# An inner Strassen level for product 5 of the first matrix multiplication, four units at a time, in the second token block of a fused MLP kernel

## The chip, the cores and the metric

The kernel runs on one core of one Trainium2 chip. Times are device microseconds (us) of that core. Each run of the kernel has a state: "slow" when the core is granted a lower clock or when the run is more than 1.5% above the fastest run of the same kernel. The medians quoted are of all runs.

Names in the profiles: PE is TensorE, which does the matrix multiplications ("matmuls"); PEld is the loading of its weights; DVE is VectorE, ACT ScalarE, POOL GpSimd, SP SyncE. A small q after a name (SPq) marks the queue of an engine. PSUM is the memory, in banks, in which the products of matmuls are summed; SBUF holds the operands. f16 and f32 are number formats of 16 and 32 bits. L625 is line 625 of that run's kernel.

A ratio of two kernels is the mean time of the fast runs of one over the mean time of the fast runs of the other in the same rounds, so it is not quite the ratio of the medians quoted beside it.

## The reference, cut to what matters

```python
B, S, D, F = 1, 2048, 1024, 3584
def reference(x, w1, b1, w2, b2):
    y = _layernorm(x, axis=-1)
    h = _gelu(jnp.einsum("bsd,df->bsf", y, w1) + b1)      # "matmul 1"
    return jnp.einsum("bsf,fd->bsd", h, w2) + b2           # "matmul 2"
```

All inputs are bf16. The kernel treats the 2048 tokens as two blocks of 1024 (block 0 and block 1).

## The kernel before

The kernel already uses Strassen's method in Winograd's form: a product of two matrices, each cut in 2x2 blocks, is made from seven block products instead of eight. In matmul 1 the blocks are halves of the token block (512 tokens), halves of K (D = 1024, so four tiles of 128), and pairs of 128-column slices of F. One such pair is a "unit" (14 units); two units are a "chunk" (7 chunks), whose weights are loaded together.

The seven products of a unit accumulate in three PSUM banks where they can. Product 5 is the odd one: it belongs to two of the four outputs, so it is copied out of PSUM once and then added twice, by `w6` and by `c7`.

```python
SEQ1 = (1, 5, 6, 2, 7, 3, 4)
OPER1 = {1: ("A11", (0, 0)), 2: ("A12", (1, 0)), 3: ("S4", (1, 1)), 4: ("A22", 4),
         5: ("S1", 1), 6: ("S2", 2), 7: ("S3", 3)}        # token operand, weight operand (number n: the sum Tn)

def w1_sums(s, c, prio):                 # T1..T4 of one chunk, on VectorE
    ...
    if n > 1:                            # T1 and T3 in one instruction of 2048 elements
        T1 = T3 = add("DVE", cost2(2 * KH * 2 * P), lambda e: e.tensor_tensor(
            out=t1_sb[:, n % 2, 0:3:2]..., in0=raw[:, :, :, 1, :], in1=raw[:, 0]..., op=ALU.subtract), ...)
    ...

def mm1_unit(s, c, v, T, t0):
    ...
    P1 = prod(1, ())                     # each prod: KH = 4 matmuls of 128x512
    o1 = snap(1, P1, b0 if fork else s1, pt[6] - SLOT)
    P5 = prod(5, ())
    o5 = snap(5, P5, s5, pt[3] - SLOT)   # product 5: PSUM -> SBUF, f32
    P6 = prod(6, (o1,))                  # bank b0: P1 + P6
    o2 = add("DVE", 0.7, lambda e: e.tensor_tensor(     # "w6": bank b5 = b0 + P5
        out=ps[:, b5.k, :], in0=ps[:, b0.k, :], in1=sn_sb[:, s5.k, :], op=ALU.add), (P6, o5), ...)
    P2 = prod(2, (o1,) if fork else ())
    ...
    P7 = prod(7, (P6, o2))               # bank b0: P1 + P6 + P7; waits for w6
    c22 = fin(7, P7, o5, s5, pt[4] - SLOT, ())          # "c7": b0 + P5
    gelu(22, sn(s5), c22, ...)
    P3 = prod(3, (o2,))                  # bank b5: output 12
    ...
    P4 = prod(4, (P7, c22))              # bank b0: output 21
```

Matmul 2 of both blocks uses a second, inner level of the same method for most of its products, with matmuls of 128x256; the change carries that idea into matmul 1. All instructions are listed first and then put in a fixed order, engine by engine, by a list scheduler in the kernel's own code. So one added instruction can move many others, and each engine then runs its queue strictly in that order.

Of the kernel before, what the change touches and what calls it, by code (L numbers as in the profile page):

```python
# [5 lines left out]
ACT = mybir.ActivationFunctionType  # L6
ALU = mybir.AluOpType
BF16 = mybir.dt.bfloat16
FP16 = mybir.dt.float16
# [14 lines left out]
P = 128  # L24
# [61 lines left out]
class Planner:  # L86
# [8 lines left out]
    def add(self, *a, **k):  # L95
        o = Op(*a, **k)
        self.ops.append(o)
        return o
# [139 lines left out]
def bass_standalone__mixer_channel_mlp__prompt_kernel(  # L238
# [24 lines left out]
    with ExitStack() as es:  # L263
# [27 lines left out]

        x16 = x_sb[:, :, :].bitcast(FP16)
        w1_16 = w1_sb[:, :, :, :].bitcast(FP16)
        h = {q: h_sb[:, n] for n, q in enumerate((11, 12, 21, 22))}
# [199 lines left out]
        def dma_T(s, i, prio, gate):  # L494
# [6 lines left out]
            y_in[(s, i)] = res  # L501

        opnd = {}
        h_war = {}
# [26 lines left out]

        cost2 = lambda n: 0.15 + n / 1920
        t1_use = {}
        SEQ1 = (1, 5, 6, 2, 7, 3, 4)
# [5 lines left out]
        def w1raw(n, kh, ev, v=None):  # L540
            t = w1_sb[:, n % N_W1, kh * KH:(kh + 1) * KH, :].rearrange("p k (v e c) -> p k v e c", v=2, e=2)
            return t[:, :, :, ev, :] if v is None else t[:, :, v, ev, :]

        def w1_sums(s, c, prio):
            n = s * NC + c
            tv = lambda k: t1_sb[:, n % 2, k - 1].rearrange("p k (v c) -> p k v c", v=2)
            ld = w1_ld[(s, c)]
            war = t1_use.get(n - 2, {})

            def tt(k, x0, x1, deps):  # L550
                return add("DVE", 0.65, lambda e: e.tensor_tensor(out=tv(k), in0=x0, in1=x1, op=ALU.subtract),  # L551
                           [*deps, *war.get(k, ())], prio + 0.5 * k, f"w1T{k}_{s}_{c}")

            if n > 1:
                raw = w1_sb[:, n % N_W1].rearrange("p k c -> p (k c)").rearrange("p (j v e c) -> p j v e c", j=2, e=2, c=P)
                T1 = T3 = add("DVE", cost2(2 * KH * 2 * P), lambda e: e.tensor_tensor(
                    out=t1_sb[:, n % 2, 0:3:2].rearrange("p a k (v c) -> p a (k v) c", c=P), in0=raw[:, :, :, 1, :],
                    in1=raw[:, 0].rearrange("p v e c -> p e v c"), op=ALU.subtract),
                    [*ld, *war.get(1, ()), *war.get(3, ())], prio + 0.5, f"w1T13_{s}_{c}")
            else:  # L560
                T1 = tt(1, w1raw(n, 0, 1), w1raw(n, 0, 0), (ld[0],))
                T3 = tt(3, w1raw(n, 1, 1), w1raw(n, 0, 1), ld)
            T2 = tt(2, w1raw(n, 1, 1), tv(1), (ld[1], T1))
            T4 = tt(4, w1raw(n, 1, 0), tv(2), (ld[1], T2))
            w1_use[n] = list(dict.fromkeys((T1, T2, T3, T4)))
            return {1: T1, 2: T2, 3: T3, 4: T4}

# [31 lines left out]

        def mm1_unit(s, c, v, T, t0):  # L600
            n = s * NC + c
# [5 lines left out]
            if not fork:  # L607
                hold.update({1: b0, 2: b1})
                b0.seeded = False
            s1, s5 = Holder(snaps), Holder(snaps)  # L610
            pt = {p: t0 + 2 * k * SLOT for k, p in enumerate(SEQ1)}
            nm = f"{s}_{u}"
            mine = {}

# [31 lines left out]

            def gelu(q, src, o, at, frees):
                f = 2 * u + q % 10 - 1
                r = h_ok[(s, q, u)] = add("ACT", 0.70, lambda e: e.activation(  # L649
                    out=h[q][:, u, :], in_=src(), func=ACT.Gelu_apprx_tanh, bias=b1_sb[:, f:f + 1], scale=1.0),  # L650
                    [o, b1c, *h_war.get((s, q), ()), *(h_head.get((q, u), ()) if s == 0 else ())], at, f"g{q}_{nm}",
                    frees=frees)
                return r
# [3 lines left out]
            o1 = snap(1, P1, b0 if fork else s1, pt[6] - SLOT)  # L657
            P5 = prod(5, ())
            o5 = snap(5, P5, s5, pt[3] - SLOT)
            P6 = prod(6, (o1,))  # L660
            o2 = add("DVE", 0.7, lambda e: e.tensor_tensor(  # L661
                out=ps[:, b5.k, :], in0=ps[:, b0.k, :], in1=sn_sb[:, s5.k, :], op=ALU.add), (P6, o5), pt[7] - SLOT,
                f"w6_{nm}")
            P2 = prod(2, (o1,) if fork else ())
# [5 lines left out]
            P7 = prod(7, (P6, o2))  # L670
            c22 = fin(7, P7, o5, s5, pt[4] - SLOT, ())
            gelu(22, sn(s5), c22, pt[4] + 4 * SLOT, (s5,))
            P3 = prod(3, (o2,))
# [5 lines left out]
            for p, k in ((5, 1), (6, 2), (7, 3), (4, 4)):  # L679
                t1_use[n].setdefault(k, []).append(mine[p])  # L680
            return list(mine.values())
# [23 lines left out]
        def flat(*a):  # L705
            return list(dict.fromkeys(o for x in a for l in x[1] for o in l))

        def uniq(*a):
            return list(dict.fromkeys(o for l in a for o in l))

# [528 lines left out]
        for s in range(NSB):  # L1239
            last = []  # L1240
            for c in range(NC):
                n = s * NC + c
                t0 = base1[s] + c * 14 * SLOT
                if n:
                    T = w1_sums(s, c, t0 - 2 * SLOT)
                    for v in range(2):
                        last += mm1_unit(s, c, v, T, t0 + v * SLOT)
                m = n + N_W1
# [88 lines left out]
```

## Time and profile before

| | before |
|---|---|
| median of 5 runs | 341.14 us (340.67 to 439.31; the run of 439.31 us is slow) |
| span of the profiled run | 338.9 us |
| TensorE (PE) busy | 332.5 us, 98% |
| VectorE (DVE) busy | 274.1 us, 81% |
| ScalarE (ACT) busy | 165.2 us, 49% |

The first lines of the profile page of the kernel before: span, then busy time, share of the span and number of instructions of each engine (PEld is the loading of weights into TensorE).

```profile
span 338.9 us, 5855 instructions
## 1 busy us (share of the span) xinstructions
PE 332.5 (98%) x2347; PEld 219.1 (65%) x2347; DVE 274.1 (81%) x350; ACT 165.2 (49%) x275; POOL 21.4 (6%) x47
```

A busy PE alone does not say that PE is the limit. The chain of work that ended last does: it is followed back from the last instruction, at each step to what released it. The columns are start, duration, and what ran; "x384" is the number of instructions merged in a line. This is the chain of the kernel before from 29.32 us on; its last two lines, 0.02 us of issue and 0.42 us of VectorE, are left out.

```profile
29.32 69.93 PE ps L625 x324
99.25 32.10 PE ps L898 x294
131.34 24.17 PE ps L823 x112
155.52 19.87 PE ps L898 x182
175.39 1.73 PE ps L625 x8
177.11 1.53 PE ps L898 x14
178.64 82.88 PE ps L625 x384
261.52 73.36 PE ps L898 x672
334.88 1.54 PE ps L903 x14
```

Each line starts where the line above ends, and in this part no other engine and no transfer appears. L625 is matmul 1 (128x512 matmuls), L898 the inner products of matmul 2 (128x256). The stage that the change touches is the line at 178.64 us: 384 matmuls in 82.88 us, 215.8 ns each. The 672 narrower ones after it take 73.36 us, 109.2 ns each. Two narrow ones cost 218.4 ns, almost the same as a wide one, so the width is nearly free and the number of multiplications sets the time.

The other engines in that stage, from the view of busy time by stretches (in brackets the number of instructions):

```profile
178.00:261.50 83.50, 83.50 (x392) 38.13 (x391) 52.83 (x64) 48.51 (x78) 0.00 (x0) 1.00 0.63 210
```

The columns after the stretch and its length are busy time of PE, PEld, DVE, ACT and POOL, then granted clock, DMA share and GB/s. VectorE is 52.83 us busy of 83.50 us.

### The profile page before, as it was taken

Reading aid. Unit: us, or ns where it says so; the run is one execution under the profiler, and the core shown is the slowest. Engines: PE = TensorE matmul, PEld = TensorE weight load, DVE = VectorE, ACT = ScalarE, POOL = GpSimd, SP = SyncE. Lnnn points to the kernel's source line nnn. Section 1 sums busy time; section 2 is a strip of 40 time slices with the busy share of each in tenths; the row PEclk is TensorE's granted clock in tenths of the full one; section 3 lists DMA queues with packets and bytes.
Section 4 is the critical chain, followed back from the end, with each engine's and each line's share of the span. In section 5 each row is a group of like instructions: output and inputs, shape, how many; then the busy total and the mean of one; then the engine's idle time right before and its main releaser. Section 6 shows DMA issues by size and latency. Waiting matters only on the chain.

```text
span 338.9 us, 5855 instructions
## 1 busy us (share of the span) xinstructions
PE 332.5 (98%) x2347; PEld 219.1 (65%) x2347; DVE 274.1 (81%) x350; ACT 165.2 (49%) x275; POOL 21.4 (6%) x47
## 2 busy tenths in 40 slices
PE   5999999999999999999999999999999999999997
PEld 4986444444458886447884444444445888888885
DVE  4789997989899989999995578387547989989954
ACT  3865975764688878212113575576475331101110
POOL 2320120000011403200000000000000000000000
PEclk9999999999999999999999999999999999999999
DMA  7739999897999999999593747949931999998112
GB/s 244 254 71 307 355 351 292 281 380 245 311 337 294 339 286 384 195 336 400 191 349 96 276 148 260 339 145 371 315 110 39 349 354 356 348 363 267 62 35 91
DMA packets 79204, 89.18 MB, mean 263 GB/s; under 512 B 14026, under 2 KB 66122, under 8 KB 78666
## 3 DMA queue, kind: packets, MB, share of 16 engines
q1 hardware_dynamic: 79034, 88.69, 81.0%
q8 instruction: 18, 0.29, 0.4%
q10 hardware_dynamic: 144, 0.13, 0.1%
q14 instruction: 8, 0.07, 0.0%
HBM read 61.81 MB, written 24.38 MB: 254 GB/s over the span
## 4 chain that ended last, share of the span: by engine, by line
PE 97%; DMA 1%; DVE 1%; ACT 0%; POOL 0%; issue 0%
PE ps L625 46%; PE ps L898 37%; PE ps L823 7%; PE ps L583 5%; PE ps L481 1%; DMA x_sb<-in_x_dram 1%; PE ps L903 0%; DVE st_sb L396 0%; ACT yw_sb L488 0%; POOL rstd_sb L403 0%; DVE x_sb L406 0%; DVE o_sb L787 0%; DVE mv_sb L399 0%; DVE vpe_sb L400 0%; PE ps L384 0%
## 5 line engine op out<-in xcount | busy, mean ns | idle before, releaser
L625 PE MATMUL ps<-yw_sb,t_sb 128*128 128x512 f16 x416 | 96.3, 379 | 0.0
L625 PE MATMUL ps<-yw_sb,w_sb 128*128 128x512 f16 x312 | 74.0, 379 | 0.0
L625 PEld LDWEIGHTS ps<-yw_sb,t_sb 128*128 128x128 f16 x416 | 40.7, 98 | 48.6
L649 ACT ACTIVATE h_sb<-ps,b_sb 128x512 f16<-128x512 f32 x76 | 50.7, 684 | 31.8 <-PE ps L625 30.5
L625 PEld LDWEIGHTS ps<-yw_sb,w_sb 128*128 128x128 bf16 x312 | 30.4, 98 | 36.1
L698 DVE TENSOR_TENSOR h_sb<-h_sb 128x2048 f16<-128x2048 f16 (+2 forms) x36 | 38.2, 1085 | 0.3 <-ACT h_sb L649 0.3
L807 ACT COPY sn_sb<-ps 128x512 f32<-128x512 f32 x27 | 15.8, 584 | 31.2 <-PE ps L898 16.3
L787 DVE TENSOR_TENSOR sn_sb<-ps,sn_sb 128x512 f32<-128x512 f32 x35 | 24.0, 687 | 7.9 <-PE ps L898 7.6
L898 PE MATMUL ps<-w2a_sb,h_sb 128*128 128x256 f16 (+1 forms) x252 | 30.1, 273 | 0.0
L807 ACT COPY ps<-sn_sb 128x512 f32<-128x512 f32 x12 | 7.0, 589 | 46.2 <-PE ps L898 45.6
L643 DVE TENSOR_TENSOR sn_sb<-ps,sn_sb 128x512 f32<-128x512 f32 x28 | 19.1, 689 | 12.3 <-PE ps L625 12.2
L661 DVE TENSOR_TENSOR ps<-ps,sn_sb 128x512 f32<-128x512 f32 x26 | 18.0, 697 | 12.7 <-PE ps L625 12.4
L898 PEld LDWEIGHTS ps<-w2a_sb,h_sb 128*128 128x128 f16 x252 | 24.7, 98 | 3.7
L787 DVE TENSOR_TENSOR o_sb<-ps,sn_sb 128x512 bf16<-128x512 f32 (+1 forms) x29 | 19.4, 669 | 6.7 <-PE ps L898 3.9
L823 PE MATMUL ps<-w2a_sb,h_sb 128*128 128x512 f16 x112 | 24.3, 379 | 0.0
L649 ACT ACTIVATE h_sb<-sn_sb,b_sb 128x512 f16<-128x512 f32 x28 | 19.9, 715 | 8.9 <-DVE sn_sb L643 8.9
L898 PE MATMUL ps<-w_sb,t_sb 128*128 128x256 f16 x196 | 23.4, 273 | 0.0
L551 DVE TENSOR_TENSOR t_sb<-w_sb,t_sb 128x1024 f16<-128x1024 bf16 x26 | 17.9, 689 | 4.4 <-PE ps L625 3.9
L898 PEld LDWEIGHTS ps<-w_sb,t_sb 128*128 128x128 f16 x196 | 19.2, 98 | 2.2
L823 PEld LDWEIGHTS ps<-w2a_sb,h_sb 128*128 128x128 f16 x112 | 10.9, 98 | 13.0 <-DMA w2a_sb<-w_sums 0.3
L638 ACT COPY sn_sb<-ps 128x512 f32<-128x512 f32 x24 | 14.1, 586 | 8.6 <-PE ps L625 8.5
L583 PE MATMUL ps<-yw_sb,w_sb 128*128 128x128 f16 x256 | 17.0, 230 | 0.3 <-ACT yw_sb L488 0.3
(107 smaller groups left out, 428.6 us busy)
## 6 DMA issues: line engine op xcount, KB each, us to landing
w_sb<-in_w_dram SPq DMA_DIRECT2D x28, 512.0 KB, 5.4
x_sb<-in_w_dram SPq DMA_DIRECT2D x21, 256.0 KB, 4.6
w_sums<-x_sb SPq DMA_DIRECT2D x21, 256.0 KB, 4.8
w2a_sb<-w_inner_sums SPq DMA_DIRECT2D x12, 448.0 KB, 8.4
x_sb<-in_x_dram SPq DMA_DIRECT2D x15, 256.0 KB, 5.4
w2a_sb<-in_w_dram SPq DMA_DIRECT2D x2, 1792.0 KB, 9.4
w_inner_sums<-w_sb SPq DMA_DIRECT2D x4, 896.0 KB, 5.1
x_sb<-w_sums SPq DMA_DIRECT2D x2, 1792.0 KB, 9.1
```

Source lines behind the costliest of these rows:

```text
L551: return add("DVE", 0.65, lambda e: e.tensor_tensor(out=tv(k), in0=x0, in1=x1, op=ALU.subtract), [*deps, *war.get(k, ())], prio + 0.5 * k, ...
L583: fn = [(lambda e, b=b, hb=hold[f], f=f, k=k, t=t: e.matmul(ps[:, hb.k, t * P:(t + 1) * P], lhsT=lhs[:, k, f * P:(f + 1) * P], rhs=yop[f"A ...
L625: fn = [(lambda e, k=k: e.matmul(ps[:, hold[p].k, :], lhsT=lhs[:, k, :], rhs=yop[yo][:, k, :], start=(first and k == 0), stop=(k == KH - 1 ...
L638: return e.copy(out=dst, in_=src) if o_.eng == "ACT" else e.tensor_copy(dst, src)
L643: return add("DVE", 0.69, lambda e: e.tensor_tensor(out=sn_sb[:, hold_s.k, :], in0=ps[:, hold[p].k, :], in1=sn_sb[:, hold_s.k, :], op=ALU. ...
L649: r = h_ok[(s, q, u)] = add("ACT", 0.70, lambda e: e.activation(out=h[q][:, u, :], in_=src(), func=ACT.Gelu_apprx_tanh, bias=b1_sb[:, f:f ...
L661: o2 = add("DVE", 0.7, lambda e: e.tensor_tensor(out=ps[:, b5.k, :], in0=ps[:, b0.k, :], in1=sn_sb[:, s5.k, :], op=ALU.add), (P6, o5), pt[ ...
L698: o = add("DVE", cost2(w * dst.shape[-1]), lambda e, k0=k0, k1=k1: e.tensor_tensor(out=dst[:, k0:k1, :], in0=a[0][:, k0:k1, :], in1=b[0][: ...
L787: plus = lambda e, out, x, y: e.tensor_tensor(out=out, in0=x, in1=y, op=ALU.add)
L807: return act(lambda e: e.copy(out=out(), in_=src()), deps, at - 5, name, **k)
L823: fn = [(lambda e, k=k, t=t: e.matmul(ps[:, banks_[t].k, :], lhsT=a[0][:, k, t * P:(t + 1) * P], rhs=b[0][:, k, :], start=(first and k == ...
L898: fn = [(lambda e, k=k, j=j: e.matmul(ps[:, bank[r].k, j * HI:(j + 1) * HI], lhsT=x[0][:, k, j * P:(j + 1) * P], rhs=y[0][:, k, :], start= ...
```

## The change

In block 1, the last six chunks are taken in three pairs. For each pair (four units, "group") product 5 is computed as one larger product with an inner Winograd level over halves of F (the two chunks), of K (two of the four tiles) and of tokens (256 of 512). Before, a group's product 5 is 4 units x 4 tiles = 16 matmuls of 128x512, which is the work of 32 of 128x256. After, it is 7 sub-products x 4 = 28 of 128x256. For this T1 of both chunks is needed earlier, four sums of T1 blocks (`gS`) and four sums of S1 blocks (`yi`, in three instructions, once) are added on VectorE, and the seven sub-products leave PSUM by five copies on ScalarE and two additions on VectorE, instead of four copies.

```diff
+        GROUPED = {(1, c): (0, (c - 1) % 2) for c in range(1, NC)}
+        LEAD = 6.0
...
-            if n > 1:
+            if n > 1 and (s, c) not in GROUPED:        # grouped chunks: T1 and T3 apart
...
+        def mm1_y_sums(s, yo, prio):                   # once: sums of the token operand S1
...
+        def mm1_group(s, c, p, yo, t0, free_y):
...
+            def tt(m, x, y, op, deps, **k):
+                return add("DVE", cost2(QK * QN), lambda e: e.tensor_tensor(out=S_(m), in0=x(), in1=y(), op=op), deps,
+                           t0 - 4 + 0.2 * m, f"gS{m}_{nm}", **k)
...
+            def sub(r, deps, first=False, frees=()):
+                (xo, dx), (yv, dy) = XO[r], Y[r]
+                fn = [(lambda e, k=k, v=v: e.matmul(
+                    ps[:, bank[r].k, v * QN:(v + 1) * QN], lhsT=xo()[:, k, v * P:(v + 1) * P], rhs=yv()[:, k, :],
+                    start=(first and v == k == 0), stop=(k == QK - 1), skip_group_check=True), ())
+                    for v in range(2) for k in range(QK)]
+                subs[r] = add("PE", CS, fn, ...)
...
+            sub(1, (), True)
+            sub(5, (), True)
+            f1 = cp(...)                               # ScalarE copies f1, k5, k2, r11, r21; VectorE additions r22, r12
+            k5 = cp(...)
+            sub(6, (f1,))
...
-            P5 = prod(5, ())
-            o5 = snap(5, P5, s5, pt[3] - SLOT)
+            if G is None:
+                P5 = prod(5, ())
+                o5 = (snap(5, P5, s5, pt[3] - SLOT),)
+            else:
+                o5 = G[1][gi]                          # w6 and c7 read the group's result
```

More of the change, by code (lines that the diff above doesn't have):

```diff
@@ L292, in bass_standalone__mixer_channel_mlp__prompt_kernel @@
         x16 = x_sb[:, :, :].bitcast(FP16)
+        sn16 = sn_sb[:, :, :].bitcast(FP16)
         w1_16 = w1_sb[:, :, :, :].bitcast(FP16)
@@ L501, in dma_T, with uniq @@
             y_in[(s, i)] = res
+        def uniq(*a):
+            return list(dict.fromkeys(o for l in a for o in l))
         opnd = {}
@@ L542, in w1raw, with w1_t1 @@
             return t[:, :, :, ev, :] if v is None else t[:, :, v, ev, :]
+        T1_of = {}
+        def w1_t1(s, c, prio):
+            n = s * NC + c
+            T1_of[(s, c)] = add("DVE", 0.65, lambda e: e.tensor_tensor(
+                out=t1_sb[:, n % 2, 0].rearrange("p k (v c) -> p k v c", v=2), in0=w1raw(n, 0, 1), in1=w1raw(n, 0, 0),
+                op=ALU.subtract), [w1_ld[(s, c)][0], *t1_use.get(n - 2, {}).get(1, ())], prio, f"w1T1_{s}_{c}")
         def w1_sums(s, c, prio):
@@ L560, in w1_sums @@
             else:
-                T1 = tt(1, w1raw(n, 0, 1), w1raw(n, 0, 0), (ld[0],))
+                T1 = T1_of.get((s, c)) or tt(1, w1raw(n, 0, 1), w1raw(n, 0, 0), (ld[0],))
                 T3 = tt(3, w1raw(n, 1, 1), w1raw(n, 0, 1), ld)
@@ L598, in mm1_plain @@
                                 f"g_{c}_{i}_{f}", frees=(hold[f],))
-        def mm1_unit(s, c, v, T, t0):
+        mm1_y = {}
+        QK, QN = KH // 2, 2 * P
+        def mm1_y_sums(s, yo, prio):
+            hold = Holder(snaps, 2)
+            flat_ = lambda: sn16[:, hold.k:hold.k + 2, :].rearrange("p a b -> p (a b)")
+            blk = lambda m: flat_()[:, m * QK * QN:(m + 1) * QK * QN].rearrange("p (k c) -> p k c", c=QN)
+            w = yop[yo].rearrange("p (j k) n -> p j k n", j=2)
+            dep = uniq(*opnd[s][yo])
+            o13 = add("DVE", cost2(2 * QK * QN), lambda e: e.tensor_tensor(
+                out=flat_()[:, 0:2 * QK * QN].rearrange("p (j k c) -> p j k c", j=2, c=QN), in0=w[:, :, :, QN:],
+                in1=w[:, 0].rearrange("p k (j c) -> p j k c", j=2), op=ALU.subtract), dep, prio, f"yi13_{s}", alloc=hold)
+            t2 = add("DVE", cost2(QK * QN), lambda e: e.tensor_tensor(
+                out=blk(2), in0=w[:, 1, :, QN:], in1=blk(0), op=ALU.subtract), (o13,), prio + 0.1, f"yi2_{s}")
+            t4 = add("DVE", cost2(QK * QN), lambda e: e.tensor_tensor(
+                out=blk(3), in0=w[:, 1, :, 0:QN], in1=blk(2), op=ALU.subtract), (t2,), prio + 0.2, f"yi4_{s}")
+            q = lambda l, j: (lambda: w[:, l, :, j * QN:(j + 1) * QN])
+            mm1_y[(s, yo)] = hold, {1: (q(0, 0), dep), 2: (q(1, 0), dep), 3: (q(1, 1), dep), 4: (lambda: blk(3), [t4]),
+                                    5: (lambda: blk(0), [o13]), 6: (lambda: blk(2), [t2]), 7: (lambda: blk(1), [o13])}
@@ new lines, in mm1_group, with cp, pl_ @@
+        def mm1_group(s, c, p, yo, t0, free_y):
+            nm = f"{p}g_{s}_{c}"
+            hold_y, Y = mm1_y[(s, yo)]
+            X, dX = {}, {}
+            for i in range(2):
+                n = s * NC + c + i
+                for l in range(2):
+                    X[(i, l)] = t1_sb[:, n % 2, 0, l * QK:(l + 1) * QK, :]
+                    dX[(i, l)] = [T1_of[(s, c + i)]]
+            hs = Holder(snaps, 2)
+            S_ = lambda m: sn16[:, hs.k:hs.k + 2, :].rearrange("p a b -> p (a b)")[
+                :, m * QK * QN:(m + 1) * QK * QN].rearrange("p (k c) -> p k c", c=QN)
+            def tt(m, x, y, op, deps, **k):
+                return add("DVE", cost2(QK * QN), lambda e: e.tensor_tensor(out=S_(m), in0=x(), in1=y(), op=op), deps,
+                           t0 - 4 + 0.2 * m, f"gS{m}_{nm}", **k)
+            x = lambda i, l: (lambda: X[(i, l)])
+            s1 = tt(0, x(1, 0), x(1, 1), ALU.add, dX[(1, 0)], alloc=hs)
+            s2 = tt(1, lambda: S_(0), x(0, 0), ALU.subtract, (s1, *dX[(0, 0)]))
+            s3 = tt(2, x(0, 0), x(1, 0), ALU.subtract, (*dX[(0, 0)], *dX[(1, 0)], s1))
+            s4 = tt(3, x(0, 1), lambda: S_(1), ALU.subtract, (s2, *dX[(0, 1)]))
+            XO = {1: (x(0, 0), dX[(0, 0)]), 2: (x(0, 1), dX[(0, 1)]), 3: (lambda: S_(3), [s4]), 4: (x(1, 1), dX[(1, 1)]),
+                  5: (lambda: S_(0), [s1]), 6: (lambda: S_(1), [s2]), 7: (lambda: S_(2), [s3])}
+            c0, c2, c5 = Holder(banks), Holder(banks, seeded=True), Holder(banks)
+            bank = {1: c0, 6: c0, 7: c0, 4: c0, 2: c2, 5: c5, 3: c5}
+            subs = {}
+            at = {r: t0 + 1.0 * k for k, r in enumerate(SEQ1)}
+            CS = 4 * MM256
+            def sub(r, deps, first=False, frees=()):
[4 more added lines that the diff above has]
+                    for v in range(2) for k in range(QK)]
+                subs[r] = add("PE", CS, fn, uniq(deps, dx, dy), at[r], f"G{r}_{nm}", alloc=bank[r] if first else None,
+                              frees=frees)
+            q = lambda h_: ps[:, h_.k, :]
+            g = Holder(snaps, 4)
+            row = lambda i, j: sn_sb[:, g.k + 2 * i + j, :]
+            def cp(out, src, deps, a, name, **k):
+                return add("ACT", 0.6, lambda e: e.copy(out=out(), in_=src()), deps, a - 3, f"{name}_{nm}", **k)
+            def pl_(dst, b, deps, a, name, **k):
+                return add("DVE", 0.69, lambda e: e.tensor_tensor(out=dst(), in0=b(), in1=dst(), op=ALU.add), deps, a - 3,
+                           f"{name}_{nm}", **k)
+            sub(1, (), True)
+            sub(5, (), True)
+            f1 = cp(lambda: q(c2), lambda: q(c0), (subs[1],), at[1], "f1", alloc=c2)
+            k5 = cp(lambda: row(1, 1), lambda: q(c5), (subs[5],), at[5], "k5", alloc=g)
+            sub(6, (f1,))
+            k2 = cp(lambda: row(0, 1), lambda: q(c0), (subs[6], k5), at[6], "k2")
+            sub(2, (f1,))
+            r11 = cp(lambda: row(0, 0), lambda: q(c2), (subs[2], k5), at[2], "r11", frees=(c2,))
+            sub(7, (k2,))
+            r22 = pl_(lambda: row(1, 1), lambda: q(c0), (subs[7], k5), at[7], "r22")
+            sub(3, (k5,))
+            r12 = pl_(lambda: row(0, 1), lambda: q(c5), (subs[3], k2), at[3], "r12", frees=(c5,))
+            sub(4, (r22,), frees=(hs, hold_y) if free_y else (hs,))
+            r21 = cp(lambda: row(1, 0), lambda: q(c0), (subs[4], k5), at[4], "r21", frees=(c0,))
+            for i, use in ((0, (subs[1], subs[2], s2, s3, s4)), (1, (subs[4], s1, s3))):
+                t1_use.setdefault(s * NC + c + i, {}).setdefault(1, []).extend(use)
+            return g, {0: (r11, r12), 1: (r22, r21)}, list(subs.values())
@@ L601, in mm1_unit @@
+        def mm1_unit(s, c, v, T, t0, G=None):
             n = s * NC + c
@@ L610, in mm1_unit, with v5, b5v @@
             s1, s5 = Holder(snaps), Holder(snaps)
+            if G is not None:
+                gi = GROUPED[(s, c)][1]
+                b5.seeded = True
+            def v5():
+                if G is None:
+                    return sn_sb[:, s5.k, :]
+                return sn_sb[:, G[0].k + 2 * gi:G[0].k + 2 * gi + 2, v * QN:(v + 1) * QN]
+            def b5v(h_):
+                return ps[:, h_.k, :] if G is None else ps[:, h_.k, :].rearrange("p (j c) -> p j c", j=2)
             pt = {p: t0 + 2 * k * SLOT for k, p in enumerate(SEQ1)}
             nm = f"{s}_{u}"
+            if G is not None:
+                pt[1] -= 3 * SLOT
             mine = {}
@@ L645, in fin, with gelu @@
                     (o, so), at, f"c{p}_{nm}", frees=frees)
-            def gelu(q, src, o, at, frees):
+            def gelu(q, src, o, at, frees, form=None):
                 f = 2 * u + q % 10 - 1
+                dst = h[q][:, u, :] if form is None else h[q][:, u, :].rearrange(form, j=2)
                 r = h_ok[(s, q, u)] = add("ACT", 0.70, lambda e: e.activation(
-                    out=h[q][:, u, :], in_=src(), func=ACT.Gelu_apprx_tanh, bias=b1_sb[:, f:f + 1], scale=1.0),
+                    out=dst, in_=src(), func=ACT.Gelu_apprx_tanh, bias=b1_sb[:, f:f + 1], scale=1.0),
                     [o, b1c, *h_war.get((s, q), ()), *(h_head.get((q, u), ()) if s == 0 else ())], at, f"g{q}_{nm}",
@@ L657, in mm1_unit @@
             o1 = snap(1, P1, b0 if fork else s1, pt[6] - SLOT)
-            P5 = prod(5, ())
-            o5 = snap(5, P5, s5, pt[3] - SLOT)
+            if G is None:
+                P5 = prod(5, ())
+                o5 = (snap(5, P5, s5, pt[3] - SLOT),)
+            else:
+                o5 = G[1][gi]
             P6 = prod(6, (o1,))
             o2 = add("DVE", 0.7, lambda e: e.tensor_tensor(
-                out=ps[:, b5.k, :], in0=ps[:, b0.k, :], in1=sn_sb[:, s5.k, :], op=ALU.add), (P6, o5), pt[7] - SLOT,
-                f"w6_{nm}")
+                out=b5v(b5), in0=b5v(b0), in1=v5(), op=ALU.add), (P6, *o5), pt[7] - SLOT,
+                f"w6_{nm}", alloc=b5 if G is not None else None)
             P2 = prod(2, (o1,) if fork else ())
@@ L670, in mm1_unit @@
             P7 = prod(7, (P6, o2))
-            c22 = fin(7, P7, o5, s5, pt[4] - SLOT, ())
-            gelu(22, sn(s5), c22, pt[4] + 4 * SLOT, (s5,))
+            if G is None:
+                c22 = fin(7, P7, o5[0], s5, pt[4] - SLOT, ())
+                gelu(22, sn(s5), c22, pt[4] + 4 * SLOT, (s5,))
+            else:
+                c22 = add("DVE", 0.69, lambda e: e.tensor_tensor(out=v5(), in0=b5v(b0), in1=v5(), op=ALU.add),
+                          (P7, o2), pt[4] - SLOT, f"c7_{nm}")
+                g22 = gelu(22, v5, c22, pt[4] + 4 * SLOT, (), "p (j c) -> p j c")
+                G[3].append(g22)
+                if len(G[3]) == 4:
+                    g22.deps += [o for o in G[3][:-1]]
+                    g22.frees = (G[0],)
             P3 = prod(3, (o2,))
@@ L679, in mm1_unit @@
             for p, k in ((5, 1), (6, 2), (7, 3), (4, 4)):
-                t1_use[n].setdefault(k, []).append(mine[p])
+                if p in mine:
+                    t1_use[n].setdefault(k, []).append(mine[p])
             return list(mine.values())
@@ L706, in flat @@
             return list(dict.fromkeys(o for x in a for l in x[1] for o in l))
-        def uniq(*a):
-            return list(dict.fromkeys(o for l in a for o in l))
         tq_ok = {r: [] for r in range(4)}
@@ L1244, in bass_standalone__mixer_channel_mlp__prompt_kernel @@
                 if n:
+                    if (s, c) in GROUPED and GROUPED[(s, c)][1] == 0:
+                        w1_t1(s, c, t0 - LEAD - 2)
+                        w1_t1(s, c + 1, t0 - LEAD - 1.9)
+                        if (s, "S1") not in mm1_y:
+                            mm1_y_sums(s, "S1", t0 - LEAD - 2)
+                        g_, ok_, subs_ = mm1_group(s, c, 5, "S1", t0 - LEAD, (s, c + 2) not in GROUPED)
+                        G = (g_, ok_, subs_, [])
+                        last += subs_
                     T = w1_sums(s, c, t0 - 2 * SLOT)
                     for v in range(2):
-                        last += mm1_unit(s, c, v, T, t0 + v * SLOT)
+                        last += mm1_unit(s, c, v, T, t0 + v * SLOT, G if (s, c) in GROUPED else None)
                 m = n + N_W1
```

## The prediction

> **What bounds the kernel now.** TensorE. The page's first part gives PE 332.5 us busy of a 338.9 us span (98%); the chain that ended last is 97% PE. Its listing in order of time has no gap in the stage concerned: 384 matmuls of 128x512 take 82.88 us from 178.64 us, 215.8 ns each, and the 672 of 128x256 after them take 73.36 us, 109.2 ns each. The Trainium skill ("TensorE: Matmul & The Clock Gate", back-to-back issue gap) states N/2.4 GHz plus about 2.5 ns when warm; this trace agrees at both widths, and the granted clock is 1.0. So halving the width costs almost nothing (2 x 109.2 = 218.4 against 215.8), and only fewer multiplications shorten the stage. From 178 to 262 us VectorE is 53.3 us busy and ScalarE 49.0 us.
>
> **What the change removes.** In block 1 six of the seven chunks, in three groups of four units, stop computing product 5 as 16 matmuls of 128x512 (16 x 215.8 ns = 3.45 us per group) and compute seven sub-products of four 128x256 matmuls (28 x 109.2 ns = 3.06 us): 0.395 us per group, 1.19 us in all. Four copies of product 5 out of PSUM per group go too (0.59 us each, mostly ScalarE).
>
> **What it adds and moves.** Per group: four 128x512 f16 sums on VectorE (estimate 0.42 us each, from 0.69 us at 1024 and 1.22 us at 2048 elements), two 0.69 us PSUM additions, two splits of the fused T1/T3 sum (0.3 us), five ScalarE copies of 0.58 us. Once: three token sums, about 1.5 us. VectorE gains about 11.6 us in all, to some 65 of 83 us; ScalarE about 0.5 us a group.
>
> **What lies on the critical path.** The PE saving wholly; the rest only where a new wait appears. By the new order of instructions, sub-products are interleaved with the preceding units' products, so nearly each has a 0.86 us product between it and what it needs. Two tight places, laid out by hand with the trace's durations:
> - First group: VectorE is never idle from 173 to 180 us in the old trace. I get the first operand sum ready about 2 us early.
> - Second and third groups: the later chunk's weights are requested when a buffer comes free, land 4 to 5 us later, and then T1 and four sums stand in VectorE's queue ahead of the "w6" additions which product 7 needs. I get 0.2 to 0.5 us of slack; a wait of up to 0.5 us per group is possible, none is my central case.
>
> The stage after is bound by PE too, so the gain should pass through.
>
> **Prediction.** 341.13 - 1.19 + 0.15 (stalls) = about 340.1 us; range 339.2 to 341.4. Faster by over 2%: 0.01; within 2%: 0.97; slower by over 2%: 0.02.
>
> **What would show it.** Right: in the chain, the same gap-free stretch with 48 matmuls of 128x512 replaced by 84 of 128x256, about 1.2 us shorter; 128x256 intervals near 109 ns; VectorE up by about 11 us there; the last stage equally long. Wrong: VectorE or ScalarE steps, or a weight load, in the chain between sub-products or before product 7, with idle PE time ahead.
>
> **What would make it wrong.** A late weight load; the in-order VectorE queue holding back w6; sub-products costing more than 109 ns per matmul at their borders; the last stage limited by transfers; scatter between runs, 0.5 us in the old one.

## The result, and the profile after

| | before | after |
|---|---|---|
| median | 341.14 us (5 runs) | 340.19 us (5 runs, 338.94 to 340.49) |
| ratio | | 0.9967, 95% interval 0.9944 to 0.9990 |
| the stage (PE chain) | 82.88 us | 81.69 us |

The page of the changed kernel begins:

```profile
span 338.5 us, 5977 instructions
## 1 busy us (share of the span) xinstructions
PE 330.9 (98%) x2383; PEld 221.8 (66%) x2383; DVE 282.4 (83%) x376; ACT 167.0 (49%) x279; POOL 22.6 (7%) x47
```

The chain that ended last in the changed kernel, from the second load wait of block 0 on. L745 is what L625 was, L1029 what L898 was, and L670 is the new sub-products.

```profile
125.23 8.04 DMA w2a_sb<-w_sums
133.27 0.05 issue
133.32 22.84 PE ps L954 x105
...
179.27 5.18 PE ps L745 x24
184.46 0.44 PE ps L670 x4
184.89 0.86 PE ps L745 x4
185.75 0.44 PE ps L670 x4
...
218.19 13.81 PE ps L745 x64
232.01 0.87 PE ps L670 x8
...
241.97 18.99 PE ps L745 x88
260.96 73.36 PE ps L1029 x672
```

The stage runs from 179.27 to 260.96 us, 81.69 us: 1.19 us less than 82.88 us. It still holds nothing but PE. A sub-product of four matmuls takes 0.44 us, two in a row 0.87 us, where 4 x 109.2 ns is 0.437 us; so a border between wide and narrow matmuls costs nothing to be seen. The last stage is 73.36 us in both kernels, so the gain passes through to the end.

The spans of the two profiled runs differ by only 0.4 us, because the stage starts at 179.27 us here and at 178.64 us in the profile before. That difference lies in block 0, where both kernels have the same instructions in the same order on every engine (the two traces first differ at 176.63 us, on VectorE); most of it is the first three lines above, a load for matmul 2 that landed late (TensorE waited 0.4 us for it). This is why the stage, and not the span of one run, is the measure in what follows.

VectorE and ScalarE in the stage of the changed kernel, same columns as before:

```profile
178.00:261.00 83.00, 83.00 (x434) 42.27 (x433) 61.72 (x90) 50.89 (x83) 0.00 (x0) 1.00 0.63 214
```

VectorE rises from 52.83 to 61.72 us, ScalarE from 48.51 to 50.89 us. These two stretches begin 0.64 and 1.27 us before the stage; between the ends of the stage itself VectorE rises from 52.27 to 60.84 us and ScalarE from 48.53 to 50.49 us. How close this comes to costing time is seen at the second group. The timeline of the changed kernel (start, duration, engine, line, operation, output and inputs), cut to VectorE and to product 7 on PE:

```profile
205.36 0.69 DVE L554 TENSOR_TENSOR t_sb<-w_sb 128x1024 f16<-128x1024 bf16 x1 [0.25 <-DMA w_sb<-in_w_dram]
206.09 0.42 DVE L652 TENSOR_TENSOR sn_sb<-t_sb 128x512 f16<-128x512 f16 x1
206.54 0.43 DVE L652 TENSOR_TENSOR sn_sb<-sn_sb,t_sb 128x512 f16<-128x512 f16 x1
206.89 0.42 DVE L652 TENSOR_TENSOR sn_sb<-t_sb 128x512 f16<-128x512 f16 x1
207.22 0.42 DVE L652 TENSOR_TENSOR sn_sb<-t_sb,sn_sb 128x512 f16<-128x512 f16 x1
207.56 1.29 DVE L785 TENSOR_TENSOR ps<-ps,sn_sb 128x512 f32<-128x512 f32 x2
...
208.94 1.89 PE L745 MATMUL ps<-yw_sb,t_sb 128*128 128x512 f16 x8
```

T1 of the later chunk waits a quarter of a microsecond for its weights, then come the four sums (0.42 us each), then the two `w6` additions (0.69 us each, overlapping). The first ends at 208.25 us, and the product 7 that needs it starts at 208.94 us: 0.69 us of slack. In the first and third groups it is 0.73 and 0.45 us.

### The profile page after: what moved, and what is told of

Read it like the earlier page. It is cut to its first block, busy times and chain, and to the rows that moved or that the text cites. A ratio compares the mean times of both kernels' runs of the same rounds, so it can differ in the third digit from the quotient of the medians.

```text
span 338.5 us, 5977 instructions
## 1 busy us (share of the span) xinstructions
PE 330.9 (98%) x2383; PEld 221.8 (66%) x2383; DVE 282.4 (83%) x376; ACT 167.0 (49%) x279; POOL 22.6 (7%) x47
## 4 chain that ended last, share of the span: by engine, by line
PE 88%; DMA 5%; SPq 3%; ACT 2%; POOL 1%; DVE 0%; issue 0%
PE ps L745 43%; PE ps L1029 33%; PE ps L954 7%; PE ps L670 3%; DMA x_sb<-in_x_dram 2%; DMA w2a_sb<-w_sums 2%; PE ps L597 2%; SPq L329 2%; SPq L498 1%; PE ps L1034 0%; ACT h_sb L420 0%; ACT h_sb L416 0%; ACT x_sb L469 0%; ACT sn_sb L938 0%; ACT ps L938 0%
## 5 line engine op out<-in xcount | busy, mean ns | idle before, releaser
L745 PE MATMUL ps<-yw_sb,t_sb 128*128 128x512 f16 x368 | 86.1, 379 | 0.0
L745 PE MATMUL ps<-yw_sb,w_sb 128*128 128x512 f16 x312 | 74.0, 379 | 0.0
L745 PEld LDWEIGHTS ps<-yw_sb,t_sb 128*128 128x128 f16 x368 | 36.0, 98 | 40.8
L745 PEld LDWEIGHTS ps<-yw_sb,w_sb 128*128 128x128 bf16 x312 | 30.5, 98 | 34.2
L938 ACT COPY sn_sb<-ps 128x512 f32<-128x512 f32 x27 | 15.8, 585 | 31.3 <-PE ps L1029 16.2
L918 DVE TENSOR_TENSOR sn_sb<-ps,sn_sb 128x512 f32<-128x512 f32 x35 | 24.0, 687 | 8.4 <-PE ps L1029 7.6
L1029 PE MATMUL ps<-w2a_sb,h_sb 128*128 128x256 f16 (+1 forms) x252 | 30.1, 273 | 0.0
L1029 PEld LDWEIGHTS ps<-w2a_sb,h_sb 128*128 128x128 f16 x252 | 24.7, 98 | 3.7
L954 PE MATMUL ps<-w2a_sb,h_sb 128*128 128x512 f16 x112 | 24.5, 379 | 0.4 <-DMA w2a_sb<-w_sums 0.4
L1029 PE MATMUL ps<-w_sb,t_sb 128*128 128x256 f16 x196 | 23.4, 273 | 0.0
L1029 PEld LDWEIGHTS ps<-w_sb,t_sb 128*128 128x128 f16 x196 | 19.2, 98 | 2.2
L758 ACT COPY ps<-ps 128x512 f32<-128x512 f32 x17 | 9.8, 574 | 13.2 <-PE ps L745 13.0
L597 PEld LDWEIGHTS ps<-yw_sb,w_sb 128*128 128x128 bf16 x256 | 15.7, 102 | 0.7 <-DMA w_sb<-in_w_dram 0.7
```

Of the source, the lines that this page charges most:

```text
L597: fn = [(lambda e, b=b, hb=hold[f], f=f, k=k, t=t: e.matmul(ps[:, hb.k, t * P:(t + 1) * P], lhsT=lhs[:, k, f * P:(f + 1) * P], rhs=yop[f"A ...
L745: fn = [(lambda e, k=k: e.matmul(ps[:, hold[p].k, :], lhsT=lhs[:, k, :], rhs=yop[yo][:, k, :], start=(first and k == 0), stop=(k == KH - 1 ...
L758: return e.copy(out=dst, in_=src) if o_.eng == "ACT" else e.tensor_copy(dst, src)
L918: plus = lambda e, out, x, y: e.tensor_tensor(out=out, in0=x, in1=y, op=ALU.add)
L938: return act(lambda e: e.copy(out=out(), in_=src()), deps, at - 5, name, **k)
L954: fn = [(lambda e, k=k, t=t: e.matmul(ps[:, banks_[t].k, :], lhsT=a[0][:, k, t * P:(t + 1) * P], rhs=b[0][:, k, :], start=(first and k == ...
```

## The experiments

The theory: the change saves 3 groups x (16 x 215.8 - 28 x 109.2 ns) = 1.19 us of TensorE time, all of it on the chain, and everything it adds on other engines is hidden in slack. Rivals: the gain comes from the changed order of instructions and from the removed copies; or it is scatter; or VectorE has so much idle time in the stage that the added vector work could be of any size.

All variants are correct. The stage is read from each profile's chain: from the first 128x512 matmul after the last 128x256 matmuls of block 0 to the first 128x256 matmul of the last stage. By the verdict at 2%, block0_one is slower and every other variant with a ratio is the same; below 2% the intervals and the stage have to decide. No stage is given for the variants of block 0, where the matmuls at the boundary of the blocks come in another order, and for after_c, whose profile is of a slow run.

| run | stage, us | median, us | before in the same rounds, us | ratio, 95% interval |
|---|---|---|---|---|
| again | 81.69 | 340.02 | 341.58 | 0.9964 (0.9939 to 0.9989) |
| pad8 | 83.00 | 341.16 | 341.58 | 1.0002 (0.9978 to 1.0026) |
| one_group | 82.48 | 340.66 | 341.58 | 0.9981 (0.9957 to 1.0004) |
| extra_dve | 83.56 | 342.24 | 341.58 | 1.0028 (1.0002 to 1.0054) |
| block0_one | | 350.83 | 341.21 | 1.0268 (1.0223 to 1.0314) |
| block0_too | | 346.45 | 341.21 | 1.0139 (1.0087 to 1.0190) |
| t2_early | 81.69 | 340.44 | 341.21 | 0.9957 (0.9920 to 0.9994) |
| before_again | 82.88 | 341.12 | | one run |
| t2_act | 81.69 | 342.20 | 341.10 | 1.0027 (0.9981 to 1.0073) |
| after_c | | 340.00 | 341.10 | 0.9957 (0.9933 to 0.9981) |
| block0_nb | | 346.48 | 341.10 | 1.0153 (1.0112 to 1.0193) |
| before_c | 82.88 | 340.81 | | one run |

### again: the changed kernel once more

> The changed kernel itself once more, for a second profile and a sharper ratio. Theory (fewer multiplications): the inner product-5 stage, from the first 128x512 f16 matmul of block 1 after the boundary to the first 128x256 matmul of the last block, is again 81.7 us and free of gaps, against 82.88 us before; total about 1.1 us faster (ratio near 0.9967). The 0.4 us wait for a second-weight load near 131 to 133 us, in code that both kernels share, need not recur. Rival (the difference is only scatter of transfers in the first block): the stage differs from 81.7 us or the ratio moves to 1.000.

The stage is 178.59 to 260.28 us, 81.69 us again. The ratio is 0.9964. The rival that calls it scatter falls: the stage is equal to the hundredth in two profiles of each kernel, while other stretches of the same runs vary by half a microsecond. The wait near 132 us did recur (0.4 us); more on that below.

### pad8: the same order and the same copies, without the saved matmuls

```diff
+                if r == 1:
+                    fn = fn + fn          # sub-product 1 computed twice, same result
                 subs[r] = add("PE", CS, fn, ...)
```

> Same order of instructions on all five engines, same copies and sums, but sub-product 1 is computed twice, so each group has 32 matmuls of 128x256 instead of 28. Theory (fewer multiplications): the stage grows by 3 x 4 x 109.2 ns = 1.31 us to about 83.0 us, and the total is 0.1 us slower than before (ratio near 1.000). Rival (the gain comes from the changed order or from the product-5 copies that went away): the stage stays near 81.7 us or at least clearly under 82.9 us, ratio near 0.997.

The chain of this run at the second group and at the end of the stage:

```profile
207.90 1.31 PE ps L670 x12
209.21 1.73 PE ps L747 x8
...
242.51 18.99 PE ps L747 x88
261.50 73.36 PE ps L1031 x672
```

Where the changed kernel has two sub-products in a row (8 matmuls, 0.87 us), this one has 12 in 1.31 us. The stage is 178.50 to 261.50 us, 83.00 us, where 83.0 us was expected, and the ratio to before is 1.0002. With the order, the sums and the copies of the change but not its saving, the gain is gone. (The intervals of the two ratios, 0.9978 to 1.0026 here and 0.9939 to 0.9989 for "again", overlap a little; the stage decides.) So the gain in the stage is the twelve saved matmuls of 128x256, 1.31 us, less the 0.12 us by which pad8, with two narrow matmuls for each wide one, is above the 82.88 us before.

### one_group: a third of the dose

```diff
-GROUPED = {(1, c): (0, (c - 1) % 2) for c in range(1, NC)}
+GROUPED = {(1, c): (0, (c - 1) % 2) for c in range(5, NC)}
```

> Only the last pair of chunks (5 and 6 of block 1) uses the inner level. Theory: saves 0.395 us, the stage is 82.88 - 0.40 = 82.48 us, with no gap. Rival (the gain is a one-off from the new order at the head of the stage): the stage is 82.9 us. In the total 0.4 us is close to the scatter, so the stage in the profile decides.

The stage is 178.94 to 261.42 us, 82.48 us: 0.40 us saved by one group, 1.19 us by three. The gain grows with the number of groups, so it is no one-off. (The total, ratio 0.9981, agrees but is within its interval of 1.)

### extra_dve: using up the slack of VectorE

```diff
+                def fn(e):
+                    if m < 2:             # before the first two operand sums of a group
+                        e.bn_stats(bs_sb[:, m, :], x_stat())
+                    return e.tensor_tensor(out=S_(m), in0=x(), in1=y(), op=op)
```

> Two statistics instructions of about 0.6 to 0.68 us each are put in front of the first two operand sums of every group on VectorE, order otherwise the same; results are unchanged. In the profile of the changed kernel the w6 additions end 0.73, 0.69 and 0.45 us before the product-7 matmuls that need them start. Theory (the added vector work is free only because of that slack): 1.2 to 1.4 us more makes product 7 wait about 0.6, 0.65 and 0.9 us, about 2.1 us in all; the stage is then near 83.8 us, above the kernel before, and the total about 1 us slower than before. Rival (VectorE has 21 us of idle time in the stage, so the extra work is absorbed): stage still near 81.7 us.

The timeline of this run at the second group, cut to the same instructions as above:

```profile
206.68 0.69 DVE L655 BATCH_NORM_STATS2 bs_sb<-t_sb 128x6 f32<-128x512 f16 x1
...
207.73 0.69 DVE L655 BATCH_NORM_STATS2 bs_sb<-t_sb 128x6 f32<-128x512 f16 x1
...
209.34 1.29 DVE L791 TENSOR_TENSOR ps<-ps,sn_sb 128x512 f32<-128x512 f32 x2
210.09 1.90 PE L751 MATMUL ps<-yw_sb,t_sb 128*128 128x512 f16 x8 [0.43 <-DVE ps L791]
```

Now product 7 has an idle time before it, ended by VectorE's L791, the `w6` addition. The stage is 179.30 to 262.86 us, 83.56 us (about 83.8 us was expected), 1.87 us more than in the changed kernel. Measured from the start of the stage, the first product-7 line of the three groups in the chain ends 0.53, then another 0.60, then another 0.73 us later than in the changed kernel (expected 0.6, 0.65 and 0.9), and the whole saving and more is lost. About 1.2 us of vector work per group (the first `w6` starts 2.70 us after the end of T1 here, 1.51 us there) cannot be absorbed, although VectorE has 21 us of idle time in the stage. What counts is not the idle time in the stage but the slack ahead of the one instruction that TensorE waits for.

### block0_one and block0_too: the same change where VectorE has no room

```diff
-GROUPED = {(1, c): (0, (c - 1) % 2) for c in range(1, NC)}
+GROUPED = {(1, c): (0, (c - 1) % 2) for c in range(1, NC)} | {(0, c): (0, (c - 5) % 2) for c in range(5, NC)}   # block0_one
+GROUPED = {(1, c): (0, (c - 1) % 2) for c in range(1, NC)} | {(0, c): (0, (c - 3) % 2) for c in range(3, NC)}   # block0_too
```

> The changed kernel with one more group: chunks 5 and 6 of block 0 too. Multiplications alone would save another 0.395 us in the first block's stage (29.3 to 99.3 us, 324 matmuls without a gap). But VectorE is already 18.7 us busy of the 21 us from 78 to 99 us there, and the group brings about 3.4 us of vector work and the token sums another 1.5 us: 23.6 of 21 us. Theory (the saving is kept only where VectorE has room): waits for VectorE appear in that stage or at the start of the next, and the first block loses 1 to 3 us; total 0.5 to 2.5 us slower than the changed kernel. Rival (only PE counts): 0.4 us faster than the changed kernel, no VectorE step in the chain.

> Both later pairs of block 0 (chunks 3 and 4, 5 and 6) grouped as well. Only PE counting, this is 0.79 us faster than the changed kernel. Theory: about 8.3 us of vector work is added to a stretch from 52 to 99 us in which VectorE has about 6 us free, so it is slower than the changed kernel, by more than the variant with one group: 1 to 5 us.

Both lose, so the rival that only TensorE counts falls. But the sizes were missed: one group lost far more (ratio 1.0268) than the expected 0.5 to 2.5 us, and more than two groups did (1.0139). In block0_one the wait that stands out is a wait of TensorE of 6.5 us for a ScalarE copy. The timeline of that run there, without most of the lines in between:

```profile
110.49 0.55 POOL L463 TENSOR_TENSOR rstd_sb<-vpe_sb,nhalf 128x1 f32<-128x1 f32 x1
110.88 1.08 DVE L832 TENSOR_TENSOR o_sb<-w2a_sb,w_sb 128x1792 f16<-128x1792 f16 x1
111.12 7.83 POOL L466 TENSOR_TENSOR st_sb<-mv_sb,rstd_sb 128x1 f32<-128x1 f32 x1
111.88 1.08 DVE L832 TENSOR_TENSOR t_sb<-t_sb,h_sb 128x1792 f16<-128x1792 f16 x1
...
117.82 1.08 DVE L832 TENSOR_TENSOR t_sb<-h_sb 128x1792 f16<-128x1792 f16 x1
118.99 1.24 ACT L469 ACTIVATE x_sb<-x_sb,st_sb,rstd_sb 128x1024 f16<-128x1024 bf16 x1 [8.13 <-POOL st_sb L466]
...
120.77 1.04 PE L1029 MATMUL ps<-o_sb,t_sb 128*128 128x256 f16 x4 [6.54 <-ACT ps L938]
```

A GpSimd multiplication of 128x1 elements, the second of its kind for block 1, took 7.83 us. In the kernel before the same one took 0.56 us, and the fastest of the eight 0.19 us. Here it started while VectorE ran a sequence of two-input instructions without a gap, and it ended within 0.1 us of that sequence. The Trainium skill ("GPSIMD Engine Reference", Specifications) says that GpSimd's interfaces to SBUF are shared with VectorE, with contention from VectorE instructions "with two SBUF inputs"; the trace agrees, and it shows the size. ScalarE's queue stood behind that multiplication for 8.13 us, and TensorE behind ScalarE for 6.54 us. In this variant a long run of VectorE sums fell on this place.

The wait was not all that was lost there. This is the stretch right after it, with the columns of the stretches above (the granted clock is the third number from the end):

```profile
121.00:126.00 5.00, 5.00 (x25) 3.59 (x24) 0.00 (x0) 3.01 (x7) 0.93 (x3) 0.50 0.81 244
```

With the clock at 0.50 for most of the time, the 28 matmuls from 120.77 to 126.58 us took 5.81 us, where 28 x 109.2 ns is 3.06 us. The wait and this stretch together are 9.3 us of the 10.4 us by which the span of this profile exceeds that of the changed kernel (348.9 against 338.5 us). That the wait lowered the clock is not shown by a run of its own.

In block0_too no GpSimd instruction from 88 to 150 us took longer than 1.27 us. Its losses are others: TensorE waits 3.1 us in two waits for the first operand sum of its two groups, each behind a weight load in the chain (7.94 and 6.58 us), and the chain then runs through VectorE's queue for several microseconds. After the longer of these waits, 2.58 us, the granted clock was again 0.50, from 75 to 78 us.

### block0_nb: is it the GpSimd multiplication?

```diff
         order = pl.place()
+        for o in [o for o in order["POOL"] if o.name.startswith("nb")]:
+            order["POOL"].remove(o)       # the 128x1 multiplication goes to ScalarE,
+            o.eng = "ACT"                 # right before its only user; nothing else moves
+            k = next(k for k, q in enumerate(order["ACT"]) if o in q.deps)
+            order["ACT"].insert(k, o)
```

The edit also writes the multiplication as a ScalarE activation with the same result, for all token tiles; the group in block 0 is that of block0_one.

> The variant with one group in block 0, with one tiny multiplication per token tile (128x1, normalisation) moved from GpSimd to ScalarE, right before its only user; every other instruction keeps its place. With the group on, one such multiplication took 7.83 us instead of 0.19 us, ending in the first gap in a run of two-input VectorE instructions, and TensorE waited 6.5 us for the ScalarE copy behind it. Theory (a crowded VectorE shuts GpSimd out of memory): about 6 to 8 us of the 9.7 us loss disappear, total near 343 to 345 us. Rival (the loss comes from the late weight load and full VectorE queue alone): it stays above 348 us.

The median fell from 350.83 us (its rounds) to 346.48 us, the ratio to before from 1.0268 to 1.0153: about 4 us regained (in other rounds, so compare the ratios), less than the 6 to 8 us expected. It fits neither the theory (343 to 345 us) nor the rival (above 348 us), and the runs spread from 344.49 to 348.23 us. The 6.5 us wait is gone from the list of waits of TensorE, and the granted clock was 1.00 from 120 to 142 us; this profile, of the fastest of the four runs, is 6.2 us shorter than that of block0_one (342.7 against 348.9 us). So the held multiplication is one cause and the largest one seen, but not the whole. In this run TensorE waits 2.5 us for a load of the second weights, which did not show in block0_one, and 0.9 us for `w6` in the added group; another GpSimd instruction took 2.89 us. What makes up each part of the rest was not taken further: no variant of block 0 came near the changed kernel.

### before_again, t2_early, t2_act, after_c, before_c: the load wait that both kernels share

In block 0, product 6 of matmul 2 needs second weights that are loaded late. In four of the first five profiles of the changed kernel and its variants TensorE waited there for 0.3 to 0.5 us (list of waits), and in the first profile of the kernel before it did not. Two questions: did the change cause it, and can it be removed?

> The kernel before once more, for a second profile of the stretch both kernels share. If the wait for the second-weight load near 132 us is scatter of transfers and no effect of the change, it appears here too in some size between 0 and 0.6 us; the product stage of block 1 is 82.88 us again.

> A third profile of the kernel before. If the later issue of the second-weight load in the changed kernel is systematic, it is again about 24.5 us after the start of block 0's second stage here and over 25.0 us in the changed kernel's profile of this call; if it is scatter, the two ranges overlap.

The stage of block 1 is 82.88 us in all three profiles of the kernel before. The load was issued 24.60 us after the start of block 0's second stage in the first profile of the kernel before, 24.54 us in before_again and 25.10 us in before_c, with a wait of TensorE of 0.2 us in the latter. In the changed kernel and its variants it was 24.99 to 25.35 us in the five profiles before t2_early. The ranges overlap, so by what was set down beforehand it is scatter. But they overlap barely: from the start of block 0's second stage to the start of block 1's stage it is 79.39, 79.40 and 79.79 us in the three profiles before, and 79.70 to 80.18 us in the five others. A loss of up to 0.4 us there, without any difference in the instructions of that stretch, is not excluded by these few profiles. The ratios do not ask for one: 0.9967, 0.9964 and 0.9957 of 341 us are 1.1 to 1.5 us, against 1.19 us from the stage, but their intervals are too wide to rule it out. This stays open.

> The changed kernel on the same chip and in the same rounds as the variant that loads from ScalarE's queue: ratio to before near 0.9965 again, stage 81.69 us.

Ratio 0.9957. The profiled run of after_c: slow (585.9 us at clock 0.564), so its profile was not used and the stage expected of it, 81.69 us, was not tested there. t2_early and t2_act, whose edits lie outside the stage, both show 81.69 us.

> The changed kernel with two transposes of block 1's tokens moved behind the second-weight load for product 6 in the queue of SyncE; nothing else changes its order. In four profiles of the changed kernel and its variants, product 6 of block 0 waited 0.4 us for that load, which had been issued 0.04 us after transposes that held the queue for 1.4 to 2.7 us. Expected: the load is issued about 3 us earlier, the wait near 132 us is gone, and the stage of block 1 starts 0.3 to 0.5 us earlier; total 0.3 to 0.5 us faster than the changed kernel (about 1.5 us, ratio 0.995 to 0.996, against the kernel before). If the later transposes then hold up block 1's token sums, it is slower instead.

```diff
-dma_T(s + 1, i, ..., ((*last, *(wf["C"] if i >= TH else ())), last))
+dma_T(s + 1, i, ..., ((*last, *(wf["C"] if i >= TH else wf["p5"] if i == 1 else ())), last))
```

This moved only one of the two transposes that I meant to move: the edit gates one half of the tile. The load was still issued only at 24.5 us, because by then its buffer had just come free: the chain of this run has 224 matmuls from 99.66 us, ending at 124.13 us, directly before the issue. The wait of TensorE for it was gone from the list, though the 112 matmuls that need it still took 24.42 us from their start to the next group, against 24.17 us in the kernel before. And a new path took over the chain, later in the same stage:

```profile
145.72 0.04 issue
145.76 7.64 DMA w2a_sb<-in_w_dram
153.41 0.02 issue
153.43 2.03 DVE w_sb L988
```

The load for another product now stands behind a row of transposes in the same queue, and a VectorE sum and a ScalarE copy behind that. Block 1 started 79.92 us after the second stage of block 0 (179.58 - 99.66), against 79.95 us in "again" (178.59 - 98.64). No gain against the changed kernel: ratio 0.9957, where that has 0.9957 to 0.9967. The ratio lies in the range expected of t2_early all the same, so here the profile decides and not the ratio; one run of the kernel before in these rounds, 345.40 us, counts as fast and helps the ratio by about 0.001.

> The changed kernel with the two second-weight loads for product 6 of block 0 issued from ScalarE's queue, just before the ScalarE copy that waits for the same sub-product anyway; every other instruction keeps its place. In five profiles of the changed kernel and its variants these loads were issued 25.0 to 25.35 us after the start of block 0's second stage, held up by transposes in SyncE's queue, against 24.5 us in two profiles of the kernel before, and TensorE then waited 0.1 to 0.6 us. Expected: issue at about 24.5 us, that wait gone, and, unlike the moved transposes, no new wait before 160 us; 0.3 to 0.5 us faster than the changed kernel. If ScalarE, which must now wait and issue, delays the copies behind it, the gain is lost there.

```diff
         order = pl.place()
+        for o in [o for o in order["SP"] if o.name.startswith("w2_0_T2")]:
+            order["SP"].remove(o)
+            o.eng = "ACT"                 # issued from ScalarE's queue, before the copy r21_5_0
+            k = next(k for k, q in enumerate(order["ACT"]) if q.name == "r21_5_0")
+            order["ACT"].insert(k, o)
```

```profile
123.77 0.33 ACTq L329
124.11 0.03 issue
124.13 11.13 DMA w2a_sb<-w_sums
135.26 0.05 issue
135.31 22.84 PE ps L954 x105
```

The loads were issued when expected, 24.49 us after the start of the stage, but the second half then took 11.13 us to land instead of 8.04 to 8.78 us in the earlier profiles that have it in their chain, and TensorE waited 2.2 us in all. The expectation was wrong: the time of issue was not what set the time of landing. Which transfers it competed with was not measured. The variant is about 2 us slower than the changed kernel by the medians of the same rounds (342.20 against 340.00 us); the intervals of the two ratios meet at 0.9981. The profile agrees: block 1 started 81.99 us after the second stage of block 0 (181.27 - 99.28), about 2 us later than in the others.

Neither variant is shown to beat the changed kernel.

## Why the prediction was right

- **The total.** Predicted 340.1 us (339.2 to 341.4); measured 340.19 us. The range also holds the median of the kernel before, 341.14 us, so the total alone is a weak test; the stage is the strong one. That the median came within 0.1 us of the forecast is partly luck: the five runs spread over 1.55 us, and the 0.15 us of stalls in the forecast did not come in the stage.
- **What bounds the kernel.** Right. The chain of the stage is nothing but TensorE in both profiles, and its length follows the count of matmuls in four kernels: 82.88 us (384 wide), 82.48 us (one group), 81.69 us (three groups), 83.00 us (three groups with eight products' worth of matmuls).
- **The saving.** Predicted 1.19 us, measured 82.88 - 81.69 = 1.19 us. The Trainium skill ("TensorE: Matmul & The Clock Gate", back-to-back issue gap) gives the form N/2.4 GHz + 2.5 ns, for what it calls the isolated gap; worked out for N = 256 that is an estimate of 109.2 ns, and the trace shows 109.2 ns, also in runs of four. pad8 shows that it is this term: without it the gain is gone.
- **What is added on VectorE.** Mis-sized. The estimate was 11.6 us; the page shows 282.4 - 274.1 = 8.3 us, the stage 60.84 - 52.27 = 8.6 us. I added up durations, but in the timeline back-to-back instructions of VectorE overlap by about 0.08 us (0.42 us long, 0.34 us apart), and VectorE has one PSUM copy of 0.7 us fewer; for 26 more instructions that makes about 2.8 us, which would account for most of the 3 us by which the estimate was too high. ScalarE gained 2.0 us in the stage against the 1.5 us predicted. Neither mattered for the time.
- **The tight places.** The right ones. First operand sum "about 2 us early": it ended at 182.26 us for a sub-product at 185.59 us, 3.3 us early. Slack of `w6` in the second and third groups "0.2 to 0.5 us": 0.69 and 0.45 us, so the second group had more than forecast (the first has 0.73 us). extra_dve showed that the slack of `w6` is a real limit.
- **Stalls of 0.15 us.** None in the stage. The wait of 0.4 us that the profile of the changed kernel does show is in block 0; a profile of the kernel before has it too, with 0.2 us.
- **The gain passes through.** Right: the last stage is 73.36 us in both.

## What to carry to other kernels

When one engine runs without a gap for a whole stage, count its instructions: the change of that count times the measured interval gave the saving to the hundredth of a microsecond, and a padded variant with the same order and copies, which lost the gain, shows that nothing else in the stage did it. Hidden work is limited by the slack in front of the particular instruction that the busy engine waits for, not by the idle share of the engine that does the work; here 21 us of idle time held less than 1.2 us of extra work per group. The same change that gains 1.2 us where VectorE is 63% busy (52.83 of 83.50 us) lost 5 to 10 us against the kernel before in block 0, where it is 89% busy (18.7 of the 21 us from 78 to 99 us). But the losses there ran through late loads, a held GpSimd instruction and a stretch at half the clock as well; that VectorE's share alone makes the difference is not shown.

## What the Trainium skill lacked or had wrong

- "TensorE: Matmul & The Clock Gate", back-to-back issue gap: it says that in a real stream of weight loads and matmuls the sustained spacing is about 131 ns at N = 512, and that N/2.4 + 2.5 over-counts there. Here 384 such pairs took 82.88 us without a gap, 215.8 ns each, so the formula that it calls isolated is the one that holds, and it holds at N = 256 too (672 pairs, 109.2 ns each).
- "GPSIMD Engine Reference", Specifications: it names the contention with VectorE instructions with two SBUF inputs, but neither it nor another page gives how long a run of several such instructions can hold one GpSimd instruction. In block0_one a 128x1 multiplication took 7.83 us, where the same one took 0.56 us in the kernel before; it ended when a gapless run of VectorE instructions did.
